# Two attention blocks on one core: another order of the projections, 128 steps of maxima ahead of the loop, sums that stay in one PSUM bank

## The chip, the core and the metric

The kernel runs on one core of a Trainium2 chip. A core has five engines that work side by side, each through its own instructions in order: PE (matrix products; its weight loads stand in the profile as PEld), DVE (vector), ACT (scalar functions and copies), POOL (a slower vector engine) and SP, which here issues the transfers. Results of PE land in PSUM, eight banks of 128 rows by 512 numbers. The metric is device time in microseconds (us): 1739.64 us, the median of three runs (1739.52 to 1739.67).

## The reference

Two independent attention blocks, A and B, on inputs of 2048 rows by 640 columns, 32 heads of 20 columns each. A looks at eight earlier rows (dilation 2) for each row; B looks at all rows:

```python
# A: idx = pos - 2 * arange(8), masked where idx < 0
qkv = (x @ wqkv) ...                                  # both blocks: [2048, 3 * 640]
logits = einsum("bhsd,bhswd->bhsw", q, kg) * scale    # A: 8 gathered keys per row
o = einsum("bhsw,bhswd->bhsd", softmax(logits), vg)   # A
scores = einsum("bhqd,bhkd->bhqk", q, k) * scale      # B: 2048 x 2048 per head
o = einsum("bhqk,bhkd->bhqd", softmax(scores), v)     # B
out = concatenate([oA @ wo_A, oB @ wo_B], axis=-1)
```

## The kernel before

**Products.** Numbers in float32 are split into a rounded part and a rest (`parts`, two instructions on two engines), and a product is three passes (`PASSES`) over five blocks of 128 rows: 15 matrix products for one output tile of 128 rows. Two products of at most 64 rows each run in the two row halves of PE at the same time; a "pair" below is such a couple, of 512 columns for B's scores and 320 for A's values and outputs.

**Before the loop.** PE first makes A's q and k (16 row tiles by 512, 256 and 512 columns), then B's k and q (40 tiles of 15 products of 512 columns), then the v of A and of B (64 tiles of 320 columns, all but the first eight and the last four in row halves). Beside the v's stand 52 steps (`LEAD`) of B's maxima. POOL begins A's attention as soon as A's first q and k rows are back from memory, paced by `a_pace`.

**B's loop.** B is worked in 32 units of 4 heads by 512 queries, each of 16 key blocks: 512 steps. A step has (1) scores, two pairs of 62 rows by 512 columns, and for each of the four tiles an exponential on ACT (tile `e`); (2) maxima for a later unit, two pairs of 60 rows by 512 columns, reduced by DVE (tile `mx`), either a pair at once or each half alone; (3) the values ("PV"), four plain-float32 products of 32 columns each side by side, which the trace shows as eight records `ps_st<-e,vb`. The maxima of a whole unit go through POOL (`mtr`) and memory and come back as two more rows of q, so that the scores are already reduced by their maximum. PV sums two steps in a bank; ACT copies the bank out (`more`, the first one of a unit `braw`), and POOL adds it to the unit's sum (`braw<-braw,more`). At a unit's end its row sums go to memory, DVE takes the reciprocal (`sm`), it comes back spread over the rows (`rb`), POOL multiplies, and the result goes to `ot_b`.

**What sets the order.** PE, ACT and DVE follow a string, `ORDER`, token by token: `S` two score halves, `M` and `N` a pair of maxima, `Y` one score half beside one half of maxima, `H` three pairs of A's output product, `V` the end of a step with its PV; the digits are PSUM banks. The last 24 steps (`TAIL`) follow a plain loop. A's attention on POOL is given out by `begin` at each `V`: POOL's instructions are added until their own estimate, `gp.us`, passes the step's number times `STEP` plus `AHEAD`. An A row tile takes four score units (multiply `akv<-akv,aq`, then adds), a softmax with two small DVE operations, four value units (multiply `akv<-akv,al`, then adds into `ao`), five transpositions on DVE (`turn<-ao`), a way through memory, and a split on POOL (`aot`); then PE can multiply it by the output weights. `after(n, ...)` puts an operation n steps later into its engine's order.

All engine instructions are issued in one helper, L71 of the kernel before and L64 of the changed one, so rows are told apart by tile names.

## Time and profile before

| | us |
|---|---|
| median of the runs | 1739.64 |
| span of the profiled execution | 1736.3 |
| up to the first PV | 458.5 |
| from the first PV to the last (512 steps) | 1229.6 |
| from the last PV to the end | 48.2 |

The profiled execution's own time is its span, 1736.3 us; the median of the runs lies 3.3 us above it. In the page, busy time is the time in which an engine has an instruction running; neighbouring instructions overlap in their ends, so the mean of one is longer than the distance from one start to the next. The records of PE end where the profiler models their end.

### The profile page before, as it was taken

The page shows a single profiled execution, that of the slowest core. Times are in us where ns is not written, and L with a number is a line of the kernel's source. Part 1 is how long each engine was busy: PE and PEld are TensorE (multiplying, and loading weights), DVE is VectorE, ACT ScalarE, POOL GpSimd, SP SyncE. Part 2 cuts the span into 40 slices and gives each one's busy share as a digit, 9 for nine tenths or more (in the row PEclk, how much of TensorE's full clock was granted, in tenths as well). Part 3 has the DMA queues.
Part 4 walks back from the last instruction along what each step waited for, and adds up shares of the span by engine and source line. Part 5 has one row for each costly group of instructions (what it writes and reads, how often), then busy time and mean ns, then how long its engine had stood idle before and what let it go on. Part 6 is the DMA issues. An engine that isn't in the chain of part 4 may idle for free.

```text
span 1736.3 us, 34687 instructions
## 1 busy us (share of the span) xinstructions
PE 1724.5 (99%) x12711; PEld 1006.0 (58%) x12711; DVE 1348.7 (78%) x1825; ACT 1338.9 (77%) x2658; POOL 1266.2 (73%) x1122
## 2 busy tenths in 40 slices
PE   9999999999999999999999999999999999999999
PEld 8988889999545544444344444444444455434569
DVE  3113223988799999999999999999999999999300
ACT  4323224232699999999999999999999999999981
POOL 0000950999899999999999999999999963544242
PEclk9999999999999999999999999999999999999999
DMA  6347878866754365345436434542643532111123
GB/s 227 119 139 239 304 261 273 259 204 187 199 151 125 96 161 153 93 136 158 135 95 173 126 119 127 170 135 88 158 143 106 147 95 61 46 36 53 33 76 113
DMA packets 194436, 248.29 MB, mean 143 GB/s; under 512 B 89309, under 2 KB 114397, under 8 KB 193273
## 3 DMA queue, kind: packets, MB, share of 16 engines
q1 hardware_dynamic: 193688, 245.41, 47.1%
q8 instruction: 100, 1.64, 0.4%
q14 instruction: 72, 0.58, 0.1%
q10 hardware_dynamic: 576, 0.66, 0.1%
HBM read 181.08 MB, written 64.91 MB: 142 GB/s over the span
## 4 chain that ended last, share of the span: by engine, by line
PE 90%; POOL 4%; DVE 2%; ACT 1%; DMA 1%; issue 1%; SPq 0%; POOLq 0%; ACTq 0%; DVEq 0%
PE ps_st L71 90%; POOL akv L71 2%; DVE mx L71 1%; ACT e L71 1%; POOL xn L71 1%; DMA stg<-wv_b 0%; SPq L71 0%; POOL ww L71 0%; POOL xl L71 0%; POOL ao L71 0%; ACT more L71 0%; DMA vb_d<-ve 0%; POOL al L71 0%; DMA s_d<-sm 0%; DMA rb<-s_d 0%
## 5 line engine op out<-in xcount | busy, mean ns | idle before, releaser
L71 DVE TENSOR_REDUCE mx<-ps_st 128x1 f32<-128x512 f32 (+1 forms) x1504 | 1227.6, 875 | 57.3 <-PE ps_st L71 47.8
L71 ACT ACTIVATE e<-ps_st 128x512 f32<-128x512 f32 x2048 | 1066.7, 627 | 30.7 <-PE ps_st L71 16.8
L71 PE MATMUL ps_st<-bk,bq 60*128 60x512 f32 x2048 | 553.4, 436 | 1.0 <-ACT ve L71 0.5
L71 PE MATMUL ps_st<-bq,bk 62*128 62x512 f32 x2048 | 548.7, 433 | 5.6 <-ACT ve L71 3.0
L71 PE MATMUL ps_st<-e,vb 128*32 128x512 f32 x4096 | 543.0, 604 | 0.4
L71 PEld LDWEIGHTS ps_st<-bq,bk 62*128 62x128 f32 x2048 | 274.8, 184 | 403.3 <-ACT e L71 246.5
L71 POOL TENSOR_TENSOR braw<-braw,more 128x512 f32<-128x512 f32 x224 | 288.2, 1287 | 85.5 <-ACT more L71 85.1
L71 PEld LDWEIGHTS ps_st<-bk,bq 60*128 60x128 f32 x2048 | 257.1, 184 | 108.7 <-DVE mx L71 61.2
L71 POOL TENSOR_TENSOR akv<-akv,aq 128x1280 f32<-128x1280 f32 x64 | 188.9, 2951 | 166.4 <-DVE w L71 166.3
L71 POOL TENSOR_TENSOR akv<-akv 128x640 f32<-128x640 f32 (+3 forms) x304 | 282.2, 928 | 14.4
L71 ACT COPY ro<-ps_st 128x320 f32<-128x320 f32 (+2 forms) x172 | 73.7, 463 | 171.1 <-PE ps_st L71 122.7
L71 PE MATMUL ps_st<-ww,xn 64*128 64x320 f32 (+1 forms) x1776 | 187.1, 309 | 0.0
L71 PEld LDWEIGHTS ps_st<-ww,xn 64*128 64x128 f32 (+1 forms) x1776 | 175.7, 186 | 14.6 <-ACT e L71 8.3
L71 PEld LDWEIGHTS ps_st<-e,vb 128*32 128x32 f32 x4096 | 82.1, 108 | 149.0 <-issue 75.4
L71 POOL TENSOR_TENSOR akv<-akv,al 128x1280 f32<-128x1280 f32 x64 | 151.6, 2368 | 0.2
L71 ACT COPY more<-ps_st 128x512 f32<-128x512 f32 x224 | 136.3, 609 | 3.5 <-PE ps_st L71 1.5
L71 PE MATMUL ps_st<-xn,w 128*128 128x512 f32 x480 | 115.8, 390 | 0.0
L71 PEld LDWEIGHTS ps_st<-xn,w 128*128 128x128 f32 x480 | 90.1, 188 | 19.3
L71 ACT CAST pr<-ps_st 128x512 fp32r<-128x512 f32 x40 | 23.5, 587 | 98.8 <-PE ps_st L71 96.0
L71 PE MATMUL ps_st<-ww,aot 64*128 64x320 f32 x960 | 99.7, 308 | 0.0
L71 DVE TENSOR_TENSOR pr<-ps_st,pr 128x512 fp32r<-128x512 f32 x40 | 27.6, 691 | 86.7 <-ACT pr L71 86.7
L71 PEld LDWEIGHTS ps_st<-ww,aot 64*128 64x128 f32 x960 | 90.3, 186 | 5.8 <-POOL ao L71 0.6
(65 smaller groups left out, 1062.5 us busy)
## 6 DMA issues: line engine op xcount, KB each, us to landing
akv<-ka_d SPq DMA_DIRECT2D x128, 320.0 KB
akv<-va_d SPq DMA_DIRECT2D x128, 320.0 KB
kb_d<-pr SPq DMA_DIRECT2D x20, 512.0 KB
qb_d<-pr SPq DMA_DIRECT2D x20, 512.0 KB
bk<-kb_d SPq DMA_DIRECT2D x16, 640.0 KB
bq<-qb_d SPq DMA_DIRECT2D x64, 160.0 KB
stg<-xb SPq DMA_DIRECT2D x16, 512.0 KB
rb<-s_d SPq DMA_DIRECT2D x128, 64.0 KB
```

Source lines behind the costliest of these rows:

```text
L71: return self.tc.keep_in_program_order(op(*a, **k))
```

## The change

- **Order ahead of the loop.** B's k and q come first (full rows). Then one sequence of 48 groups in row halves (`f_tokens`, 30 pairs each): B's v (16 groups of 320 columns), and A's q, k and v together as 1920 columns in pieces of 512, 512, 512 and 384 (32 groups; the weights are brought in twice, for two column blocks of x each). Beside them stand 128 steps (`LEAD`) of maxima as whole pairs, two of them to every 15 narrow pairs, three to every 15 of A's. The splits of A's weights and x use POOL for the rest.
- **A's attention** starts with the loop; nothing of it is issued before. `STEP` is 2.32 instead of 2.36. The five transpositions of a row tile are issued 1 to 5 steps after the tile is handed over (which is one A unit after its last sum), instead of 20 to 24.
- **PV** adds up the 16 steps of a unit in one bank; ACT copies the bank once, into a fixed place (`misc`). The additions on POOL go. The reciprocal of the row sums is issued 3 steps after the load it needs, instead of 7 or 8.
- **Loop.** All 512 steps follow a new `ORDER`, with `F` for one pair of an output group (A's 16 groups, then the first 4 of B's 16). Eight places hold exponentials instead of six. The maxima of 384 steps are left for it, 1158 `Y` and 189 `M` in the first 480 steps; before, 460 steps of maxima.
- **Tail.** Eight more groups of B's output and the last eight tiles follow the last PV. The last unit's row sums are spread by one product with a selection matrix and inverted in PSUM's full width on DVE.

The order in which the built programs have their instructions shows it at three places. First POOL, where A's attention begins. Before, right behind the constants (`mask`, `ve`, `neg`, `zero`):

```order
L71 AFFINE_SELECT mask<-mask 128x256
L71 MEMSET ve 128x347 x4
L71 MEMSET neg 64x128
L71 MEMSET zero 7x640
L71 TENSOR_TENSOR akv<-akv,aq 128x1280
L71 TENSOR_TENSOR akv<-akv 128x2x320
L71 TENSOR_TENSOR akv<-akv 128x2x160
```

In the changed kernel, behind the splits of A's last weights and the eighth unit of maxima:

```order
L64 TENSOR_TENSOR w<-stg,w 128x3x128
L64 TENSOR_TENSOR akv<-stg,akv 128x2x128
L64 TENSOR_TENSOR w<-stg,w 128x3x64
L64 TENSOR_TENSOR akv<-stg,akv 128x2x64
L64 CAST mtr<-mtr 128x32
L64 TENSOR_TENSOR mtr<-mtr 128x32
L64 TENSOR_TENSOR akv<-akv,aq 128x1280
L64 TENSOR_TENSOR akv<-akv 128x2x320
```

All 64 score units and 64 value units of A now stand behind the eighth unit's maxima, which end the work ahead of the loop.

Second ACT, in the middle of the loop, over a unit's end. Before (`e` are exponentials, `more` and `braw` the copies out of PV's bank):

```order
L71 COPY more<-ps_st 128x512
L71 ACTIVATE e<-ps_st 128x512 x6
L71 COPY more<-ps_st 128x512
L71 ACTIVATE e<-ps_st 128x512 x8
L71 COPY more<-ps_st 128x512
L71 ACTIVATE e<-ps_st 128x512 x8
L71 COPY braw<-ps_st 128x512
```

In the changed kernel (exponentials into `pbuf` and `big`, eight of each in turn):

```order
L64 ACTIVATE pbuf<-ps_st 128x512 x8
L64 ACTIVATE big<-ps_st 128x512
L64 COPY misc<-ps_st 128x512
L64 ACTIVATE big<-ps_st 128x512 x7
L64 ACTIVATE pbuf<-ps_st 128x512 x8
L64 ACTIVATE big<-ps_st 128x512 x8
```

One copy for 64 exponentials is left of eight.

Third DVE, around an A row tile's transpositions in the changed loop:

```order
L64 TENSOR_REDUCE mx_6419<-ps_st 128x2
L64 STREAM_TRANSPOSE turn<-ao 128x128
L64 TENSOR_REDUCE mx_6419<-ps_st 128x1 x4
L64 STREAM_TRANSPOSE turn<-ao 128x128
L64 TENSOR_REDUCE mx_6419<-ps_st 128x1 x2
L64 STREAM_TRANSPOSE turn<-ao 128x128
L64 TENSOR_REDUCE mx_6419<-ps_st 128x1 x3
L64 STREAM_TRANSPOSE turn<-ao 128x128
L64 TENSOR_REDUCE mx_6419<-ps_st 128x1
L64 TENSOR_REDUCE mx_6419<-ps_st 128x2
L64 RECIPROCAL sm<-sm 128x16
```

They stand between the reductions of the maxima, as before, about one to a step; but the first is now issued one step after the tile is handed over.

The diff, cut to what the prediction speaks of (of the two `ORDER` strings a line or two):

```diff
-LEAD = 52
-TAIL = 24
+LEAD = 128
+NP = 8
...
-STEP = 2.36
+STEP = 2.32
...
+    def p_tile(t):
+        s = t % NP
+        v = pbuf[:, s].bitcast(F32) if s < 4 else pside[0][:, (s - 4) * 1024:(s - 3) * 1024]
+        return v.rearrange("p (r c) -> p r c", r=2)
...
+    def m_pair(n):
+        m = m_two()
+        for r in range(2):
+            m_matmul(*m[1:], r, psb[:, n + r])
+        m_reduce(*m[1:], None, n)
+        m_done(m)
...
+        after(2, sp.dma_start, sm, s_d[0].rearrange("j (p c) -> j p c", c=16))
+        after(5, dve.reciprocal, sm, sm)
+        after(6, sp.dma_start, s_d[1].rearrange("j (p c) -> j p c", c=16), sm)
+        after(7, bcast)
+        after(9, gp.tensor_tensor, raw, raw, misc[:, 512:], ALU.mult)
+        if then:
+            after(10, then)
+        else:
+            after(11, out)
...
+    def b_pv(i, ns):
+        u, kb = divmod(i, NKB)
+        if kb == 0:
+            accs[u] = psb[:, ns[0]]
+            acc_n[0] = ns[0]
+        acc = accs[u]
+        for j in range(GH):
+            pe.matmul(acc[32 * j:32 * j + 32, :], vs[u // NQC][:, kb, j * VC:j * VC + 32], P[i][j % 2][:, j // 2],
+                      start=(kb == 0), stop=(kb == NKB - 1))
+        del P[i]
+        if kb == NKB - 1:
+            raw = misc[:, :512]
+            act.copy(raw, accs.pop(u))
+            if u < NU - 1:
+                normalize(raw, u, (lambda: out_last(u % NQC, raw)) if u // NQC == NG - 1 else None)
...
-            while any(u[1] >= 4 and v_rows[0] <= u[0] for u in UNITS[n:n + 3]) or c == 4 and len(done_a) > 1:
+            while c == 4 and len(done_a) > 1:
...
-            job(turn_jobs, 20 + k, part, k)
+            job(turn_jobs, 1 + k, part, k)
...
-        if ready_a or not turned or turned[0][0] > now[0]:
+        if not turned or turned[0][0] > now[0] or f_done[0] < turned[0][1] // 2 * 2:
...
+    def f_tokens(lhs, rhs, n, ns):
+        for second in range(2):
+            for k in range(KC):
+                for i, (wi, xi) in enumerate(PASSES):
+                    for r in range(2):
+                        w = r ^ second
+                        rows = slice(r * HALF, r * HALF + HALF)
+                        pe.matmul(psb[:, ns[w], :n], lhs(w, xi, k)[rows], rhs(wi, k)[rows],
+                                  start=(second == 0 and k == 0 and i == 0), stop=(second == 1 and k == KC - 1 and i == 2))
+                    yield
...
+    def oa_group(p, half, ns):
+        assert ready_a[0] >= 2 * p + 2, (p, ready_a)
+        yield from f_tokens(lambda w, xi, k: aot[w][:, xi, k], lambda wi, k: WO[half][wi][:, k], 320, ns)
...
+    for ms in ((5, 6, 7, 8), (9, 0), (1, 2), (3, 4)):
+        for n in range(NQC):
+            for m in ms:
+                if g1 < 4:
+                    p = first[g1]
+                else:
+                    p = bank()
+                    kq_matmuls(p, m, n, range(KC))
+                kq_end(p, m, n)
+                tick()
...
+    groups = [lambda ns, n=n, h=h, a=a: v_group(n, h, a, ns) for n in range(4) for h in range(2) for a in range(2)]
+    groups += [lambda ns, gi=gi, n=n, a=a: a_group(gi, n, a, ns) for gi in range(8) for n in range(gi // 4 * 2, gi // 4 * 2 + 2) for a in range(2)]
...
+    for e in range(0, len(groups), 2):
+        wd = 320 if e < 16 else A_COLS[(e - 16) // 4 % 4 + 1] - A_COLS[(e - 16) // 4 % 4]
+        two = [groups[e + o]((2 * o, 2 * o + 1)) for o in range(2)]
+        for second in range(2):
+            for o in range(2):
+                for k in range(3 * KC):
+                    if k in ((0, 8) if e < 16 else (0, 5, 10)):
+                        m_pair(4 + 2 * (m_next[0] % 2))
+                        spend(0.228)
+                    next(two[o])
+                    spend(0.0135 + wd * 0.000417)
+                if second:
+                    next(two[o], None)
...
+    f_left = [lambda ns, p=p, h=h: oa_group(p, h, ns) for p in range(NT // 2) for h in range(2)]
+    f_left += [lambda ns, qc=qc, a=a, h=h: ob_group(qc, a, h, ns) for qc in range(NQC - 1) for a in range(2) for h in range(2)]
...
-        acc = accs[u]
-        for j in range(GH):
-            pe.matmul(acc[32 * j:32 * j + 32, :], stacks[g][2][:, kb, j * VC:j * VC + 32], P[i][j % 2][:, j // 2],
-                      start=(part == 0), stop=(part == 1))
-        del P[i]
-        if part == 0:
-            return
-        del accs[u]
-        if n == 0:
-            raws[u] = sb.tile([128, 512], F32, tag="raw", bufs=3, name="braw")
-            act.copy(raws[u], acc)
-        else:
-            more = spare[n % 2][:, n // 2 % 2]
-            act.copy(more, acc)
-            after(2, pool, raws[u], raws[u], more, ALU.add)
-        give(acc)
-        if kb == NKB - 1:
-            last = g == NG - 1
...
-        if done_a and done_a[0][0] <= 0 and len(turned) + len(turn_jobs) < 2 and not loads and i > 10:
+        if done_a and done_a[0][0] <= 0 and len(turned) + len(turn_jobs) < 2 and not loads:
             a_turn(*done_a.pop(0)[1:])
         turn_parts()
         gp.us = max(gp.us, (i - 1) * STEP)
-        while i >= A_FROM and gp.us < i * STEP + AHEAD:
...
-        "Y07S61M2Y45V0Y71S26M3Y05V7Y06M3S52Y71V0Y26M3S75VY71M5S24S03N17V2Y06S15Y34VM0S74Y56V3Y70S21N46VY70M4S12S63N07V1"
...
+        "Y10Y23S45M6S10M2S45M6S10M2S45V1S67Y04Y23VS56M3S70VM5S23S47VS02M5Y43VY07S25Y46VY03M5S72VY40Y37S25VY64Y03S72V"
...
+        "F50FFFFY34FFY26FFFY37FFY42FFFY36Y74Y23FFY67FFFY42FFY36FFFY74FFM2FFFM6VS45M2Y60Y74VY25Y63S70VY42Y56S37VY04Y52"
...
+        if kind == "F":
+            if group is None:
+                group = f_left.pop(0)(ns)
+                f_at = 0
+            next(group)
+            f_at += 1
+            if f_at == 6 * KC:
+                next(group, None)
+                group = None
+        elif kind == "V":
+            begin(i)
+            b_pv(i, ns)
...
-    loop[1] = False
-    for i in range(NS - TAIL, NS + LAG):
-        begin(i)
-        if i < NS:
-            b_qk(i)
-        if i % 2:
-            b_pv(i - LAG - 1)
-            b_pv(i - LAG)
-            if fill:
-                fill.pop(0)()
...
+    whole[0] = True
+    while due or f_left:
         tick()
-        if fill:
-            fill.pop(0)()
-    pairs = [wide(), wide()]
-    last = [p for j in range(2) for w in pairs for p in (w[:, j], bank())]
...
+    pe.matmul(end[7], ident, raw, start=True, stop=True)
+    for n in range(1, 7):
+        out_matmuls(n, range(KC - 1))
+    dve.reciprocal(misc[:, 512:], end[7])
+    dve.tensor_tensor(raw, raw, misc[:, 512:], ALU.mult)
+    out_rows(qc, raw, (sp, act))
+    out_matmuls(7, range(KC - 1))
+    parts(chunk(OB[qc], 0, KC - 1), chunk(OB[qc], 1, KC - 1), ob_raw[qc][:, :512])
...
```

More of the change, by code (lines that the diff above doesn't have):

```diff
@@ L292, in attention_pair @@
     tick()
[L293 to L296 removed]
+    for k in range(KC):
+        xb_piece(1, k, 1)
     tick()
[L298 to L304 removed]
+    ident = const.tile([128, 128], F32, name="ident")
     gp.memset(ident, 0.0)
@@ L1165, in attention_pair @@
[L1165 to L1169 removed]
+        if f_left and (len(f_left) > 4 or ob_ready[0] == qc):
+            fb = [n for n in range(8) if n != acc_n[0]]
+            for _ in f_left.pop(0)(fb[len(f_left) % 3 * 2:len(f_left) % 3 * 2 + 2]):
+                pass
```

1238 lines of the change are left out of this document (525 added, 713 removed).

## The prediction

> **What bounds the kernel now.** I read the page's first part, then the windows by stage, then who waits for PE's banks, then PE's own starts.
>
> ```profile
> span 1736.3 us, 34687 instructions
> PE 1724.5 (99%) x12711; PEld 1006.0 (58%) x12711; DVE 1348.7 (78%) x1825; ACT 1338.9 (77%) x2658; POOL 1266.2 (73%) x1122
> ```
>
> PE's 99% is a record of modelled ends. The stages say more (columns: window, length, then busy time and count of PE, PEld, DVE, ACT, POOL, granted clock, share of DMA, GB/s):
>
> ```profile
> 0.00:458.00 458.00, 453.20 (x3309) 398.51 (x3311) 210.89 (x229) 140.44 (x255) 221.87 (x199) 1.00 0.68 219
> 458.00:1688.00 1230.00, 1226.51 (x9102) 563.55 (x9102) 1134.20 (x1590) 1189.90 (x2385) 1034.10 (x914) 1.00 0.41 116
> 640.00:1400.00 760.00, 759.32 (x5654) 342.64 (x5656) 740.65 (x1031) 741.93 (x1491) 735.52 (x638) 1.00 0.47 134
> 1688.00:1736.00 48.00, 44.80 (x308) 43.92 (x300) 3.60 (x7) 8.54 (x19) 10.20 (x10) 1.00 0.36 110
> ```
>
> The loop's edges are the first and last start of PV (count, shortest/median/longest in ns, first to last start):
>
> ```profile
> L71 PE MATMUL ps_st<-e,vb x4096: 592/593/619, 458.5 to 1688.1; 128*32 128x512 f32 x196
> ```
>
> So 458.5 us lie ahead, 1229.6 in it, 48.2 behind. Ahead of the loop and behind it PE alone is full (weight loads 87% and 92% busy). In the middle of the loop DVE, ACT and POOL are all 97% busy: four engines at their limit, and the clock is full. The waits there (640 to 1400; in total, times, longest):
>
> ```profile
> PEld ps_st L71 <- ACT e L71: 211.1, 341, 0.9
> PEld ps_st L71 <- DVE mx L71: 116.7, 241, 0.9
> ...
> PEld ps_st L71 <- POOL ao L71: 0.6, 2, 0.3
> ```
>
> PE takes turns waiting for banks that ACT and DVE must empty, never over 0.9 us; for POOL next to never. What PE needs if it never waits comes from distances between starts. Full rows of 512 and of 256 columns (windows, PE alone), the narrow mix, then a stretch of the loop (start, length, operation):
>
> ```profile
> 160.00:260.00 100.00, 100.00 (x440) 1.00 0.83 286
> 70.00:90.00 20.00, 20.00 (x168) 1.00 0.50 142
> ```
>
> ```profile
> 350.05 0.64 PE L71 MATMUL ps_st<-bk,bq 60*128 60x512 f32 x4
> 350.52 1.93 PE L71 MATMUL ps_st<-ww,xn 64*128 64x320 f32 x24
> 352.29 0.60 PE L71 MATMUL ps_st<-ww,xl 64*128 64x320 f32 x6
> 352.73 0.66 PE L71 MATMUL ps_st<-bk,bq 60*128 60x512 f32 x4
> ...
> 849.41 1.07 PE L71 MATMUL ps_st<-e,vb 128*32 128x512 f32 x8
> 850.40 0.50 PE L71 MATMUL ps_st<-bk,bq 60*128 60x512 f32 x2
> 850.75 0.62 PE L71 MATMUL ps_st<-bq,bk 62*128 62x512 f32 x3
> 850.99 0.45 PE L71 MATMUL ps_st<-bk,bq 60*128 60x512 f32 x1
> 851.37 1.07 PE L71 MATMUL ps_st<-e,vb 128*32 128x512 f32 x8
> ```
>
> 440 products of 512 columns in 100 us are 0.227 each, 168 of 256 in 20 us 0.119. From 350.05 to 352.73, 2.68 us, pass two pairs of 512 and 15 of 320: with 0.228 a wide pair, a narrow one takes (2.68 - 0.46) / 15 = 0.148. PV takes 0.99 (849.41 to 850.40). The pair behind it takes 0.35 and the one ahead of the next PV 0.38, where neighbours stand 0.24 apart: about 0.2 more per PV.
>
> So the loop before needs of PE: scores 512 x 0.456 = 233, maxima 460 x 0.456 = 210, PV 512 x 1.19 = 609, A's outputs 480 x 0.148 = 71, other products 30: 1153 us. It took 1229.6, 1.066 times as much.
>
> **The change part by part.** *Ahead of the loop.* PE's need is B's k and q 600 x 0.227 = 136, B's v 480 pairs x 0.148 = 71, A's 720 pairs of 512 x 0.228 = 164 and 240 of 384 x 0.174 (between the two widths) = 42, maxima 128 x 0.456 = 58: 471. By the same rows the kernel before needs 435 of its 458.5 (A's q and k 240 x (0.227 + 0.119 + 0.227) = 138, B's 136, 62 tiles of v 137, maxima 24), so 24 are start and stalls. I keep these 24: 495, **37 later**. Of this 76 x 0.456 = 35 are maxima brought forward; the loop gets them back. DVE's 256 reductions lie beside PE:
>
> ```profile
> L71 DVE TENSOR_REDUCE mx<-ps_st 128x2 f32<-128x1024 f32 x544 | 657.0, 1216 | 31.5 <-PE ps_st L71 29.8
> L71 DVE TENSOR_REDUCE mx<-ps_st 128x1 f32<-128x512 f32 x960 | 619.8, 681 | 25.8 <-PE ps_st L71 18.0
> L71 ACT COPY more<-ps_st 128x512 f32<-128x512 f32 x224 | 136.3, 609 | 3.5 <-PE ps_st L71 1.5 <-POOL braw L71 1.4 <-issue 0.2
> L71 ACT ACTIVATE e<-ps_st 128x512 f32<-128x512 f32 x2048 | 1066.7, 627 | 30.7 <-PE ps_st L71 16.8 <-ACT e L71 0.3
> ```
>
> 657.0 / 544 = 1.21 each: three in 15 wide pairs are 3.6 us against PE's 4.1, hidden; beside 384 columns PE has 3.3, so DVE sets those 16 stretches, 5 us, inside the 24. A's weights are brought in twice, 4.9 MB more beside some 100 MB in that window (219 GB/s), and asked for a group or more ahead, 8 us: nothing, unless a transfer comes later than that, which then costs its lateness.
>
> *Copies and sums of PV.* ACT loses 224 copies (136.3 us, 0.27 a step), POOL 224 additions (below). If all of ACT's copies were on the path they would be worth 136 us; if PE never waits for what they delay, nothing. ACT's load falls from 2.39 to 2.15 us a step (4 x 1066.7 / 2048, and the rest), DVE's maxima from (960 x 0.646 + 440 x 1.21) / 488 = 2.36 to (1158 x 0.646 + 189 x 1.21) / 480 = 2.03. Both cease to bind at 2.40. I take their worth as less waiting where nothing else binds: half of the 6.6%.
>
> *A's attention on POOL* is the term that decides:
>
> ```profile
> L71 POOL TENSOR_TENSOR braw<-braw,more 128x512 f32<-128x512 f32 x224 | 288.2, 1287 | 85.5 <-ACT more L71 85.1
> L71 POOL TENSOR_TENSOR akv<-akv 128x640 f32<-128x640 f32 (+3 forms) x304 | 282.2, 928 | 14.4
> L71 POOL TENSOR_TENSOR akv<-akv,aq 128x1280 f32<-128x1280 f32 x64 | 188.9, 2951 | 166.4 <-DVE w L71 166.3
> L71 POOL TENSOR_TENSOR akv<-akv,al 128x1280 f32<-128x1280 f32 x64 | 151.6, 2368 | 0.2
> L71 POOL TENSOR_TENSOR ao<-ao,akv 128x640 f32<-128x640 f32 x48 | 75.0, 1563 | 2.0
> L71 POOL TENSOR_TENSOR braw<-braw,rb 128x512 f32<-128x512 f32 x32 | 41.1, 1285 | 29.4 <-DMA rb<-s_d 25.1 <-ACT e L71 4.1 <-issue 0.2
> L71 POOL TENSOR_TENSOR aot<-back,aot 128x640 fp32r<-128x640 f32 x16 | 24.9, 1559 | 1.3
> L71 POOL TENSOR_TENSOR ao<-akv 128x640 f32<-128x640 f32 x16 | 24.9, 1559 | 0.5
> L71 POOL TENSOR_TENSOR al<-al,am 128x256 f32<-128x256 f32 x32 | 23.6, 739 | 0.0
> L71 POOL TENSOR_TENSOR al<-akv 128x64 f32<-128x64 f32 x64 | 20.5, 321 | 4.8
> ```
>
> 288 us go, but the 222 us that POOL had done by 458 now start with the loop. In the changed program A's first multiplication stands at step 4 and its last at step 364. Between them POOL has 282 + 189 + 152 + 75 + 25 + 24 + 21 of A's attention, 22 of 32 normalizations (28), 14 of 16 splits (32 with their casts) and some 25 in small ones: 850 us, **2.36 a step**. From 640 to 1400 it did 735.5 in 760 us, 97%; at that rate the 360 steps take 878, 2.44 each, slower than the 2.40 of before. PE needs only 2.16 there (scores 0.456, 0.8 x 0.456 of maxima, PV 1.19, 12 groups x 30 x 0.148 over 364 steps). POOL can hold PE up in two ways: `F` groups stand 4 to 30 steps behind the split of their second tile, and DVE's transpositions, issued 1 to 5 steps after the handover, wait for POOL's `ao` with the maxima behind them, whose banks PE wants. Before, 20 steps hid that. So I let POOL set these steps: 9 us for the first four, then 878.
>
> *The other 148 steps.* The loop's PE need is 233 + 175 (384 steps of maxima) + 609 + 600 x 0.148 = 1106; 785 of it falls in the first 364 steps, so 321 are left, 70 of them in the last 32 steps, which have no maxima. 251 x 1.033 + 70 = 329.
>
> *Tail.* Eight groups of 30 products (240 x 0.148 = 36) and eight tiles of 15 (18) are 54, the selection product 1 (PV's 0.99 is also plain float32 over 512 columns), and 3 as in the 48.2 of before, 44.8 of it products: 58, 10 more. DVE's reciprocal grows from 16 numbers to 512:
>
> ```profile
> L71 DVE RECIPROCAL sm<-sm 128x16 f32<-128x16 f32 x32 | 7.8, 243 | 1.3 <-DMA sm<-s_d 1.3
> L71 DVE RECIPROCAL am<-am 128x32 f32<-128x32 f32 x16 | 5.5, 343 | 0.0
> ```
>
> 100 ns for 16 more numbers make 3.3 us for 512 (an estimate); with the transfer behind it this lies beside 7 x 12 products, 12 us. Without that cover the tail is up to that 3.3 longer.
>
> *Sum.* 495 + 9 + 878 + 329 + 58 = 1769 us of span against 1736. The median lay 3.3 above the span; with 3 more, **1772 us**, 1.9% slower.
>
> [...]
>
> **The rivals.** *POOL doesn't bind* (18%). For it: before, PE's weight loads waited 0.6 us for POOL in 760 although POOL was just as full, and A's last `F` groups stand 20 steps or more behind their splits. Then the loop takes PE's 1106 at the old loss: 1179, and 495 + 1179 + 58 + 3 = 1735, 0.3% faster. Against it: POOL's 2.36 a step is above the 1179 / 512 = 2.30 that this gives; it decides from where POOL's work a step passes PE's pace.
>
> *PE hardly waits at all* (4%). With ACT at 2.15 and DVE at 2.03 the loop falls to PE's need: 1106, in all 1662. It wants POOL out of the way too, 2.36 a step.
>
> *Waits pile up on DVE* (16%). Two waits of DVE for POOL stand in the whole trace before, 2.85 us each:
>
> ```profile
> DVE am L71 <- POOL al L71: 5.7, 2, 3.8
> ```
>
> If each of 16 row tiles costs one of these, less the 1.2 us that a pair in the next banks covers, 16 x 1.65 = 26 come on top: 1798. [...]
>
> *The change isn't what it says* would be a lead in which DVE, not PE, sets the pace; its price is the 5 us above, and it stays inside the forecast.
>
> **How the numbers follow.** Forecast 62%: 1772, its own range 1754 (POOL at its full 850) to 1790. Rivals 18, 4 and 16%. The range 1733 to 1794 takes in the first rival's 1735 and leaves out the second and half of the third, 12%. Under 0.2% (3.5 us) this kernel's measurement tells nothing. Faster: 11 of the first rival's 18 and the second, 15%; same: 7 and 2 of the forecast, 9%; slower 76%.
>
> **What would show it.** Right: first PV near 495; POOL over 95% busy from there for some 360 steps, ending near 1385; PE's span per step about 2.4 in that time and about 2.2 behind it; DVE waiting for POOL (`turn`, `am`) and PEld for DVE or POOL's `aot` in waits longer than 0.9 us; ACT and DVE below 90%; 58 us behind the last PV. Wrong: POOL with gaps while PE runs at 2.3 or less a step (the first rival), a first PV far from 495 (PE's need mis-sized, or a transfer late in the lead), or PE's long waits on transfers.

## The result: 1842.3 us, 5.9% slower

The changed kernel takes 1842.34 us (median of four runs, 1841.33 to 1843.40), the kernel before beside it 1739.58: a ratio of 1.0593, with a 95% interval of 1.0578 to 1.0608. The prediction said 1772, and 1794 at most. The profile after, first its page:

```profile
span 1839.8 us, 35673 instructions
PE 1741.9 (95%) x13253; PEld 989.4 (54%) x13253; DVE 1370.9 (75%) x1915; ACT 1216.3 (66%) x2410; POOL 974.3 (53%) x898
```

PE is no longer full. The stages of the changed kernel (columns as in the prediction), cut at the first and last PV:

```profile
0.00:508.00 508.00, 491.26 (x4033) 421.31 (x4033) 369.37 (x357) 129.65 (x263) 81.45 (x107) 0.99 0.51 161
508.00:1781.00 1273.00, 1195.97 (x8858) 514.87 (x8858) 994.85 (x1552) 1076.92 (x2126) 885.36 (x783) 0.96 0.48 134
1781.00:1839.00 58.00, 54.69 (x370) 53.18 (x362) 6.71 (x7) 9.72 (x22) 7.51 (x8) 0.99 0.28 90
518.50:1455.00 936.50, 864.06 (x6302) 368.31 (x6304) 765.25 (x1202) 770.10 (x1514) 835.21 (x726) 0.95 0.57 159
```

```profile
L64 PE MATMUL ps_st<-pbuf,vb x2048: 592/593/1062, 508.5 to 1779.5; 128*32 128x512 f32 x187
...
L64 PE MATMUL ps_st<-big,vb x2048: 592/616/1063, 513.0 to 1781.3; 128*32 128x512 f32 x187
```

508.5 us lie ahead of the loop (before 458.5), 1272.8 in it (1229.6), 58.5 behind it (48.2). In the loop every engine has gaps, POOL too: 835 us busy in the 936.5 from A's first to its last multiplication, 89%. And the granted clock is 0.96 where it was 1.00. What DVE waited for in the loop (total, times, longest), and behind it the row for `sm` in the loop of the kernel before:

```profile
DVE mx L64 <- PE ps_st L64: 119.1, 217, 2.3
DVE sm L64 <- DMA sm<-s_d: 106.8, 7, 33.1
DVE w L64 <- DMA stg<-wo_a: 8.8, 2, 7.0
DVE turn L64 <- POOL ao L64: 6.4, 2, 4.2
```

```profile
DVE sm L71 <- DMA sm<-s_d: 0.5, 1, 0.5
```

The long wait is one that the prediction doesn't name: the reciprocal of the row sums waits for their load, with the maxima queued behind it. Two of the seven waits (15.1 and 33.1 us) lie in the last 32 steps, where no maxima are left, and cost nothing. The other five are 58.7 us, at the ends of units 3, 7, 11, 15 and 19, which are the ends of head groups (four units each).

Here is one, in SP's queue at the end of unit 3, whose last PV starts at 663.7 and whose copy starts at 664.9:

```profile
660.61 1.50 SPq L64 DMA_DIRECT2D big<-kb_d  x4
662.21 2.39 SPq L64 DMA_DIRECT2D last<-qb_d  x4
669.46 1.63 SPq L64 DMA_DIRECT2D last<-mdr  x2
675.00 2.83 SPq L64 DMA_DIRECT2D last<-qb_d  x4
...
680.83 0.56 SPq L64 DMA_DIRECT2D s_d<-misc  x1
...
684.49 2.84 SPq L64 DMA_DIRECT2D sm<-s_d  x1
```

At the end of each head group four loads of keys (`big<-kb_d`) for a later group are asked for. The issue records name eight semaphores in turn, 192 issues for each of seven of them and 191 for the eighth, and here a transfer waits for the one issued eight before it: the first key load's last update is at 669.44 and the issue eight behind it at 669.46, the third's at 674.94 and that issue at 675.00. The four key loads hold their semaphores for 9 to 15 us (660.6 to 669.5 for the first, 661.8 to 676.6 for the fourth), and the query loads (`last<-qb_d`) behind them theirs for up to 15. The store of the row sums (`s_d<-misc`), one step behind the unit's end, is asked for 16 us after the copy's start, the load behind it at 684.49, and the reciprocal starts at 690.97.

The five ends are not all alike. At units 7, 15 and 19 the store leaves 15.0, 7.9 and 11.6 us after the copy's start, at all others, unit 11 too, 0.6 to 6. At units 11, 15 and 19 the store itself is slow: the load, which waits for it, is asked for 10 to 11 us behind it, at other units 1.7 to 6.5. Unit 15, where SP waits 9.2 us for the store:

```profile
1169.41 0.55 SPq L64 DMA_DIRECT2D s_d<-misc  x1
...
1180.10 0.32 SPq L64 DMA_DIRECT2D sm<-s_d  x1
```

So the key loads make the sums late in two ways: they hold the semaphores that SP needs, and a store issued close behind two of them takes long (10 to 11 us at these three units). In the first run below, where they stand elsewhere, the load follows the store in 1.7 to 2.8 us at these three units.

PE at the same place (start, length, operation, idle time ahead and its releaser), and the stages around it:

```profile
674.87 1.07 PE L64 MATMUL ps_st<-pbuf,vb 128*32 128x512 f32 x8
...
678.10 0.40 PE L64 MATMUL ps_st<-last,big 62*128 62x512 f32 x1
691.83 0.79 PE L64 MATMUL ps_st<-big,last 60*128 60x512 f32 x1 [13.32 <-DVE mx L64]
...
693.68 1.94 PE L64 MATMUL ps_st<-big,vb 128*32 128x512 f32 x8
```

```profile
680.00:684.00 4.00, 0.00 (x0) 0.00 (x0) 0.00 (x0) 0.00 (x0) 0.65 (x1) 0.58 0.81 201
684.00:688.00 4.00, 0.00 (x0) 0.00 (x0) 0.00 (x0) 0.00 (x0) 3.84 (x3) 0.50 0.99 292
...
696.00:698.00 2.00, 2.00 (x14) 0.57 (x12) 1.59 (x2) 1.19 (x2) 0.48 (x1) 0.58 0.87 313
698.00:700.00 2.00, 2.00 (x18) 0.65 (x14) 2.00 (x5) 1.05 (x3) 2.00 (x2) 1.00 0.13 33
```

PE stands for 13.3 us from 678.5 on. The granted clock (the third figure from a row's end) is 0.58 on average from 680 to 684 and 0.50 behind, so it fell to half some 2 us after PE's last product. The next PV takes 1.94 instead of 1.07. Full speed is back some 6 us after PE has resumed.

**All stops together.** I took PE's products between each two PV's at the prediction's prices as the need of a step (steps count from 0 at the first PV). They add up to 1103 us in the loop (the prediction has 1106), so 170 us are waits. Seven stops, with the slow step behind each, make 90 of them: steps 69, 133, 197, 261 and 324 (the five reciprocals) 16.6, 13.0, 7.8, 13.4 and 17.7, in sum 68.5 (the expectations below have 13.5 and 18.6 for the last two, and so 69.5); steps 3 to 5, where DVE waits for A's output weights, 15.8; step 188, where a transposition waits for POOL's `ao`, 5.8. The other 80 are 7.3% of the need, spread as before (84 of 1146, 7.3% too).

### The profile page after: what moved, and what is told of

It is laid out like the page before. It is cut to its first block, busy times and chain, and to the rows that moved or that the text cites. A ratio compares the mean times of both kernels' runs of the same rounds, so it can differ in the third digit from the quotient of the medians.

```text
span 1839.8 us, 35673 instructions
## 1 busy us (share of the span) xinstructions
PE 1741.9 (95%) x13253; PEld 989.4 (54%) x13253; DVE 1370.9 (75%) x1915; ACT 1216.3 (66%) x2410; POOL 974.3 (53%) x898
## 4 chain that ended last, share of the span: by engine, by line
PE 71%; POOL 12%; DMA 7%; DVE 4%; issue 3%; ACT 2%; SPq 1%; POOLq 0%; ACTq 0%; DVEq 0%
PE ps_st L64 71%; POOL akv L64 9%; DVE mx L64 3%; DMA s_d<-misc 2%; DMA last<-qb_d 1%; DMA sm<-s_d 1%; POOL ao L64 1%; SPq L64 1%; DMA vb_d<-ve 1%; ACT big L64 1%; POOL al L64 1%; POOL big L64 1%; DMA akv<-va_d 0%; DVE w L64 0%; ACT pbuf L64 0%
## 5 line engine op out<-in xcount | busy, mean ns | idle before, releaser
L64 PE MATMUL ps_st<-big,last 60*128 60x512 f32 x2048 | 628.5, 433 | 41.0 <-DVE mx L64 40.5
L64 PE MATMUL ps_st<-last,big 62*128 62x512 f32 x2048 | 605.3, 437 | 37.5 <-DVE mx L64 33.5
L64 ACT ACTIVATE pbuf<-ps_st 128x512 f32<-128x512 f32 x1024 | 543.6, 630 | 93.5 <-PE ps_st L64 86.4
L64 ACT ACTIVATE big<-ps_st 128x512 f32<-128x512 f32 x1024 | 538.5, 637 | 92.5 <-PE ps_st L64 87.1
L64 PEld LDWEIGHTS ps_st<-last,big 62*128 62x128 f32 x2048 | 296.6, 188 | 505.7 <-ACT big L64 140.2
L64 PE MATMUL ps_st<-w,big 64*128 64x320 f32 (+3 forms) x3264 | 379.2, 336 | 12.8 <-ACT ve L64 8.8
L64 PEld LDWEIGHTS ps_st<-w,big 64*128 64x128 f32 (+1 forms) x3264 | 317.7, 188 | 46.3 <-ACT ve L64 9.9
L64 PEld LDWEIGHTS ps_st<-big,last 60*128 60x128 f32 x2048 | 285.8, 187 | 86.1 <-DVE mx L64 52.7
L64 PE MATMUL ps_st<-big,vb 128*32 128x512 f32 x2048 | 278.4, 617 | 0.0
L64 PE MATMUL ps_st<-pbuf,vb 128*32 128x512 f32 x2048 | 274.5, 609 | 0.5 <-DVE mx L64 0.4
```

Of the source, the lines that this page charges most:

```text
L64: return self.tc.keep_in_program_order(op(*a, **k))
```

## The experiments

The first four runs were to tell whether the stops are the whole loss and whether POOL binds behind them.

**Key loads 10 steps later.**

```diff
-                after(1 + d // 2, fn)
+                after(11 + d // 2, fn)
```

> The changed kernel with the four loads of the next key group (big<-kb_d, asked for 1 and 2 steps after a group's last score) moved 10 steps later; nothing else. Theory T: SP's queue is held by these four loads, the row sums' store and load come behind them, and DVE's reciprocal, issued 3 steps after the load, stops the maxima and with them PE at units 3, 7, 11, 15 and 19; those five stops cost 16.6 + 13.0 + 7.8 + 13.5 + 18.6 = 69.5 us beyond PE's need (half-speed clock behind each included), so 1842 - 70 = 1772 (1766 to 1782), and the waits DVE sm <- DMA sm<-s_d of the first 480 steps fall from 58.7 us to under 5. Theory P (POOL sets the pace of A's part): POOL was busy 835 of the 936.5 us from A's first to last multiplication; at the 97% of the kernel before that is 863, so at best 1842 - 73 = 1769: not told apart here. Theory Q (the queue is late whatever the key loads do): 1842 +- 5, waits as before.

Measured: 1803.56 us, ratio 1.0374 (1.0357 to 1.0392): 39 us gained where theory T has 70. The waits of the reciprocal are gone as T says, but ACT has a new one. DVE to 1640 us, then ACT from 1000 to 1345:

```profile
DVE sm L64 <- DMA sm<-s_d: 4.6, 2, 3.6
```

```profile
ACT misc L64 <- DMA ot_b<-misc: 13.9, 2, 7.0
...
ACT misc L64 <- DMA last<-qb_d: 2.9, 1, 2.9
```

The key loads now stand ahead of the store of the finished rows (`ot_b<-misc`). There is one place for the copy of PV's sums, so the next unit's copy waits for that store, and PE for the bank. The stops at steps 207, 271 and 335 cost 8.4, 9.5 and 4.2 us beyond the need, and 5.6 are left at 69. So the cause is as T has it, and the gain that T expects was too high, since the wait moves on.

**Reciprocal 3 steps later.**

```diff
-        after(5, dve.reciprocal, sm, sm)
-        after(6, sp.dma_start, s_d[1].rearrange("j (p c) -> j p c", c=16), sm)
-        after(7, bcast)
-        after(9, gp.tensor_tensor, raw, raw, misc[:, 512:], ALU.mult)
+        after(8, dve.reciprocal, sm, sm)
+        after(9, sp.dma_start, s_d[1].rearrange("j (p c) -> j p c", c=16), sm)
+        after(10, bcast)
+        after(12, gp.tensor_tensor, raw, raw, misc[:, 512:], ALU.mult)
```

> The changed kernel with the reciprocal of the row sums 3 steps later (6 steps after its load instead of 3) and what follows it 3 steps later as well; the key loads stay where they are. T: each of the five waits for the row sums (14.6, 11.0, 6.0, 12.4, 14.7 us) loses what 3 steps take, about 7 us: 24.6 of 58.7 us stay; 34 us of waits and some 5 us of slow clock go: 1842 - 39 = 1803 (1793 to 1812). P: the time doesn't fall below 1769, no other difference. If the reciprocal's place in DVE's order has nothing to do with the stops: 1842 +- 5.

Measured: 1828.99 us, 1.0508 (1.0488 to 1.0528): 13 gained, not 39. The reciprocal's waits in the first 480 steps fall to 30.4 us in five (24.6 were expected); but the finished rows now leave 3 steps later and run into the next unit's copy (step 207: ACT stands 8.8 us ahead of its copy).

**Output weights split later.** Key loads as in the first run, and:

```diff
-    loads += wide_pieces(wo_a, WO, 1, 2, dve.tensor_copy)
+    loads += wide_pieces(wo_a, WO, 1, 12, dve.tensor_copy)
```

> k_later, and in it the second half of A's output weights split on DVE 12 steps after their load instead of 2. T: the stop at steps 3 to 5 (15.8 us, two waits DVE w <- DMA stg<-wo_a of 8.8 us, two slowed splits, slow clock) goes too: 1772 - 16 = 1756 (1748 to 1766). P: POOL then holds the loop at about 863 us for A's part: not below 1769.

Measured: 1799.84 us, 1.0354 (1.0339 to 1.0370). 4 us, not 16: DVE no longer waits for the load, but the splits themselves are slow (steps 15 and 16, where they stand now, lose 6.6 us). Where the rest of the 16 went was not found. In the changed kernel's DVE, first the place where they stood:

```profile
515.97 0.49 DVE L64 CAST w<-stg 128x640 fp32r<-128x640 f32 x1 [1.88 <-DMA stg<-wo_a]
...
525.41 3.04 DVE L64 CAST w<-stg 128x640 fp32r<-128x640 f32 x1 [6.95 <-DMA stg<-wo_a]
528.48 2.04 DVE L64 TENSOR_TENSOR w<-stg,w 128x640 fp32r<-128x640 f32 x1
...
532.17 0.31 DVE L64 CAST w<-stg 128x320 fp32r<-128x320 f32 x1
```

and in this run, DVE and then POOL:

```profile
539.58 2.12 DVE L64 CAST w<-stg 128x320 fp32r<-128x320 f32 x1
541.73 1.74 DVE L64 TENSOR_TENSOR w<-stg,w 128x320 fp32r<-128x320 f32 x1
```

```profile
538.60 2.92 POOL L64 TENSOR_TENSOR akv<-akv,aq 128x1280 f32<-128x1280 f32 x1
```

The same cast of 320 columns takes 0.31 us at one time and 2.12 at another; the slow one starts under a POOL multiplication and ends 0.2 us after it (541.52). The slow cast of 640 columns in the changed kernel, 525.41 to 528.45, likewise starts under a multiplication (525.22 to 528.10) and ends 0.35 us after it. What holds the casts up there, no run shows.

**POOL lightened**, on top of this run:

```diff
-        pool(v, v, L[:, 2 * c:2 * c + 2].unsqueeze(3).to_broadcast([128, 2, H, DH]), ALU.mult)
+        gp.us += 2.37
```

> k_wo without A's 64 multiplications of values by weights on POOL (akv<-akv,al, 151 us; A's half of the output is then a sum of plain values), every other instruction in the same order and the pacing estimate unchanged. T (POOL doesn't bind): the same as k_wo within 5 us. P: POOL's 835 us fall to 684, so A's part is no longer held at 863 us: 25 to 70 us faster than k_wo.

Measured: 1789.15 us, 1.0288 (1.0272 to 1.0303): 10.7 us faster than with all of POOL's work. Neither theory's number. POOL costs something, but isn't the pace.

**Key loads by ACT.** If SP's queue is the trouble, another engine should ask for them.

```diff
-            sp.dma_start(k[r * HALF + r0:r * HALF + r0 + n].bitcast(F32), kb_d[s0:s0 + n, ...])
+            (act if g > 2 else sp).dma_start(k[r * HALF + r0:r * HALF + r0 + n].bitcast(F32), kb_d[s0:s0 + n, ...])
```

> The changed kernel with the four loads of each later key group (from the fourth on) asked for by ACT instead of SP, at the same place in the program. Theory T2: SP lets at most some eight transfers be under way, so slow key loads keep everything behind them in SP's queue; moved later (k_later) they delayed the store of the finished rows, for which the next unit's copy of PV's sums waits because there is one place for it. Off SP's queue they delay neither: waits DVE sm <- DMA sm<-s_d of the first 480 steps under 6 us, no stop at steps 69, 133, 197, 261, 324 nor at 207, 271, 335: 1842 - 69 = 1773 (1766 to 1785). If the queue is slow by itself (or the transfers only share bandwidth): the stops stay, 1800 or more.

Measured: 1840.71 us, 1.0582 (1.0567 to 1.0598): no gain, theory T2 missed by 68 us. What ACT and its queue did at the end of unit 3, and what DVE waited for to 1700 us:

```profile
667.90 0.29 ACTq L64 DMA_DIRECT2D big<-kb_d  x1
668.24 1.58 ACT L64 ACTIVATE pbuf<-ps_st 128x512 f32<-128x512 f32 x3 [6.47 <-DMA ot_b<-misc]
671.59 11.44 ACTq L64 DMA_DIRECT2D big<-kb_d  x2
683.13 2.06 ACT L64 ACTIVATE pbuf<-ps_st 128x512 f32<-128x512 f32 x4 [13.31 <-DMA big<-kb_d]
```

```profile
DVE sm L64 <- DMA sm<-s_d: 10.5, 4, 7.5
```

Of the reciprocal's waits, 58.7 us in the first 480 steps, 10.5 are left: taking the key loads out of SP's queue removes most of them. But now ACT stands still in asking, with its exponentials behind. The eight semaphores are shared by the queues of this program (in the changed kernel's tail, from 1833.17 to 1836.19, eight issues of SP and ACT by turns take the eight once round), so that the wait belongs to whoever asks next. The 6.5 us are for a store that SP had asked for (`ot_b<-misc`); some 11 of the 13.3 us lie in ACT's queue between two key loads (the 11.44 from 671.59), for a key load that ACT itself had asked for. What is left of the reciprocal's waits is mostly unit 15 (7.5 us), where the store leaves 2 us after the copy's start and the load comes 11.6 us behind it: the slow store again.

**Key loads spread out**, at 2, 6, 10 and 14 steps:

```diff
-                after(1 + d // 2, fn)
+                after(2 + 4 * d, fn)
```

> The changed kernel with the four loads of the next key group 2, 6, 10 and 14 steps after the group's last score instead of 1, 1, 2 and 2, still by SP. T2: one slow load at a time holds SP up for a few us only: 1780 (1768 to 1797). If it is the amount that the loads move and not their standing together: as k_later, about 1803, or worse.

Measured: 1804.94 us, 1.0369 (1.0354 to 1.0385). As the second theory has it (about 1803): that they stand apart is worth no more than moving them together. Stops stay at steps 69 (11.1), 207 (6.0) and 324 (6.2).

**ACT for the key loads, and two repairs elsewhere.**

```diff
-    loads += wide_pieces(wo_a, WO, 1, 2, dve.tensor_copy)
+    loads += wide_pieces(wo_a, WO, 1, 6, None, gp)
-        after(1, sp.dma_start, vb_d[s * 128:(s + 1) * 128, half * 16 * VC:half * 16 * VC + c], ve[:, :c])
+        after(1, act.dma_start, vb_d[s * 128:(s + 1) * 128, half * 16 * VC:half * 16 * VC + c], ve[:, :c])
```

> k_act, and with it the second half of A's output weights split by ACT and POOL, 6 steps after the load, instead of DVE, 2 steps after (no split of DVE stands beside a multiplication of POOL any more), and the stores of B's v ahead of the loop asked for by ACT instead of SP. T2: the stop at steps 3 to 5 goes (16 us) and the stop at 201 to 212 us of the lead, where ACT waits for a store of v (10 us with its slow clock): 1773 - 26 = 1747 (1737 to 1762). The first PV comes at about 498 us instead of 508. If POOL sets the pace: not below 1769.

Measured: 1848.45 us, 1.0625 (1.0607 to 1.0643), 101 above T2, with ACT's stops as in the run with the key loads on ACT. The two repairs do what they were meant to: the stop at steps 3 to 5 is gone (22 us of waits in the first 32 steps fall to 13), and the first PV comes at 504.2 instead of 508.5.

**One part of the change alone, in the kernel before**: the reciprocal 3 to 4 steps after its load.

```diff
-            normalize(..., *((2, 3) if last else (5, 8)), ...)
+            normalize(..., *((2, 3) if last else (5, 4)), ...)
```

> The kernel before with one part of the change: the reciprocal of the row sums 3 to 4 steps after its load instead of 7 to 8. T2: here the sums are stored 5 steps after a unit's end, not 1, so behind the key loads anyway; by the trace of before the reciprocal would come about 2 us after the load is asked for at units 11, 15, 19, 23 and 24 and 5 us or more elsewhere: at most five waits of up to 4 us, 1740 + 5 = 1745 (1739 to 1760). If the short distance alone made the changed kernel's stops: 1739 + 60 or more.

Measured: 1752.47 us against 1739.39, 1.0075 (1.0058 to 1.0093). The trace has the wait that the kernel before had not (two of its three waits, 6.8 and 4.1 us, lie ahead of maxima):

```profile
DVE sm L71 <- DMA sm<-s_d: 11.5, 3, 6.8
```

So the short distance alone costs 13 us there, for 10.9 us of waits that count; this is inside T2's range (1739 to 1760) and far from the 60 us more of the other theory. That it costs more in the changed kernel may be because the sums are also stored 1 step after the unit's end and no longer 5, with the key loads just ahead; no run moved the store alone.

**Key loads behind the finished rows** (SP again; with the two repairs of x1):

```diff
-                after(1 + d // 2, fn)
+                after(15 + d // 2, fn)
```

> x1 with the key loads back on SP, but 14 steps later than in the changed kernel: behind the store of the finished rows of their unit and ahead of the next unit's copy. Theory T3 (the transfers share eight places in turn whichever engine asks; a key load holds its place for 9 to 16 us, and the engine that asks for the eighth transfer after it waits): here only A's loads stand behind the key loads. No stop at steps 69, 133, 197, 261, 324 nor at 207, 271, 335: 1842 - 69 - 13 (what x1 shows for steps 0 to 31 and the lead) = 1760 (1750 to 1775). If the loads only push the wait on to whatever stands next in the queue: 1785 or more. P (POOL sets the pace): not below 1769.

> y1 without A's 64 multiplications of values by weights on POOL (151 us; A's half of the output is then a sum of plain values), the order unchanged. T3: what k_wo_light showed, about 11 us (5 to 16) below y1, from waits of POOL's late results, none of them long. P: POOL was the pace: 25 us or more below y1.

> y1 with the reciprocal of the row sums 5 steps after its load instead of 3 (what follows it 2 steps later as well) and the key loads 2 steps later still. T3: as y1 or up to 6 us faster, if single waits for row sums are left in y1: 1757 (1745 to 1775). If the later store of the rows runs into the next unit's copy: up to 20 us slower than y1.

Measured: y1 1808.91 us (1.0401, 1.0378 to 1.0424), y1_light 1787.49 (1.0277, 1.0262 to 1.0292), y5 1800.02 (1.0353, 1.0336 to 1.0370). T3 misses by 49 us: the loads push the wait on again, to the reciprocal of the next unit (steps 149, 213, 277, 341). y1's DVE to 1640 us:

```profile
DVE sm L64 <- DMA sm<-s_d: 34.9, 7, 10.3
```

y5 misses its 1757 by 43. And with POOL lightened y1 is 21 us faster, twice the 11 of T3 and short of the 25 of P, though y1 has no fewer waits than k_wo (144 us beyond the need of its steps, k_wo 133). What POOL's load costs depends on what else stops the loop.

**Time for both places.** Reciprocal 7 steps after the load, key loads as in the first run, x1's repairs, and a second place for the copy. In z1 its room came from the eighth exponential buffer, in u1 from the third buffer of v and outputs:

```diff
-NP = 8
+NP = 7
-            raw = misc[:, :512]
+            raw = misc[:, :512] if u == NU - 1 else pside[0][:, 3072 + u % 2 * 512:3584 + u % 2 * 512]
```

> x1's splits of the output weights and stores of v; the key loads on SP 10 steps later, as in k_later; the reciprocal of the row sums 7 steps after its load instead of 3, and what follows it 4 steps later as well; and two places in turn for the copy of PV's sums instead of one (seven exponential buffers instead of eight make the room). Theory T4: SP's queue is late by up to 16 us once in every group, wherever the key loads stand (k_later, k_spread and y1 only moved the stop to the next one in the queue that has little time), and the changed kernel stops because two things in it have little time: the reciprocal 3 steps behind its load, and the one place of the copy. With both given time the stops go: 1842 - 91 + 6 (a stop for POOL's ao stays) - 4 = 1753 (1744 to 1766), DVE's waits for sm of the first 480 steps under 4 us. If the queue's lateness itself is what costs (the loads of q or k come too late for PE): 1780 or more.

> z1 without A's 64 multiplications of values by weights on POOL (A's half of the output is then a sum of plain values). T4: POOL's load made y1 21 us slower only through SP's queue, which waits for buffers that POOL holds, and so through late row sums; with time for these it is worth 8 us or less: z1 - 4 (z1 - 8 to z1 + 2). P: POOL sets the pace: z1 - 20 or more.

> z1 with the transpositions of A's rows 3 to 7 steps after the handover instead of 1 to 5. The third rival (DVE waits for POOL's ao): 6 us of such waits are in the changed kernel's trace, so z1 - 6 (z1 - 10 to z1 - 2). If they are hidden: z1 +- 2; if the later rows reach the output groups late: up to 10 us more.

Measured: z1 1931.35 us (1.1091, 1.1074 to 1.1107), z1_light 1928.08, z1_t 1942.98. No step in z1's first 480 is over 5 us beyond its need, but its seventh buffer as the last one slowed every step. PE's weight loads waited for exponentials 422 us in these two rows (the changed kernel, in its loop: 301):

```profile
PEld ps_st L64 <- ACT pbuf L64: 237.2, 306, 3.5
PEld ps_st L64 <- ACT big L64: 185.3, 235, 2.3
```

The time of this run can't tell T4 from the rest; its room was taken at the wrong place. At that slower pace POOL's load costs next to nothing (3 us, inside the spread of z1's runs, 1927 to 1931), and later transpositions cost 12.

```diff
-    ones = [sb.tile([128, 16 * VC + 16], F32, tag="r", bufs=3, name="ve") for _ in range(3)]
+    ones = [sb.tile([128, 16 * VC + 16], F32, tag="r", bufs=2, name="ve") for _ in range(2)]
-            raw = misc[:, :512]
+            raw = misc[:, :512] if u % 2 else sb.tile([128, 512], F32, tag="raw", bufs=1, name="raw")
```

> z1 with eight exponential buffers again, as in the changed kernel; the room for a second place of the copy comes from the buffers of v and of the outputs (two instead of three), which can cost some us ahead of the loop. T4 (the stops come from the two places with little time, the reciprocal 3 steps behind its load and the one place of the copy): loop 1272 - 85 = 1187 (1180 to 1198) from first to last PV, in all 1753 (1744 to 1768), DVE's waits for sm of the first 480 steps under 4 us. If the queue's lateness itself costs: 1780 or more.

> u1 without A's 64 multiplications of values by weights on POOL (A's half of the output is then a sum of plain values). T4: POOL's load cost y1 21 us only by way of SP's queue and late row sums; here they have time: u1 - 5 (u1 - 10 to u1 + 2). P (POOL sets the pace): u1 - 20 or more.

Measured: u1 1814.18 us (1.0429, 1.0411 to 1.0446), u1_light 1772.95 (1.0198, 1.0183 to 1.0214). The two differ by 41 us, and all that differs in them is POOL's work. Of u1, DVE to 1700 us and the window of A's part; of u1_light, the same two views:

```profile
DVE turn L64 <- POOL ao L64: 31.4, 9, 8.1
```

```profile
521.70:1431.50 909.80, 872.72 (x6346) 371.80 (x6344) 765.75 (x1205) 777.73 (x1530) 840.91 (x731) 0.97 0.56 163
```

```profile
DVE turn L64 <- POOL ao L64: 3.6, 1, 3.6
```

```profile
521.70:1382.30 860.60, 846.81 (x6276) 360.40 (x6274) 757.31 (x1196) 768.95 (x1516) 691.95 (x667) 0.99 0.59 172
```

The smaller buffers cost 8 us ahead of the loop in both (first PV at 512.3; x1 504.2). In u1 the reciprocals hardly wait any more, 2.2 us in the first 480 steps. In their place DVE's transpositions wait for POOL, nine times, 31.4 us. A's part takes 910 us with POOL 92% busy, and 861 when POOL has 149 us less to do. So T4 falls in its second half: with time at the two places *these* stops are gone, and behind them POOL's work holds the loop after all.

**Is it the transpositions' place, or POOL's pace?**

```diff
-            job(turn_jobs, 1 + k, part, k)
+            job(turn_jobs, 4 + k, part, k)
```

> u1 with the transpositions of A's rows 4 to 8 steps after the handover instead of 1 to 5. T5 (what is left in u1 is the forecast's third rival: DVE's transpositions wait for POOL's ao, 31.4 us in nine waits of up to 8.1 us, with the maxima behind them): 3 steps are some 7 us, so nearly all of these waits go, and with the half-speed clock behind each about 1.3 times as much: 1814 - 40 = 1774 (1765 to 1785), near u1_light's 1773. P (POOL's pace itself): the rows then come late to the output groups instead, PE waits for POOL's splits: 1800 or more.

Measured: 1824.90 us, 1.0493 (1.0453 to 1.0533), 11 slower than u1. T5 falls. DVE's waits for `ao` shrink to 8.4 us, and PE's own grow from 1.2 to 33.6. PE and then DVE, to 1440 us (`big` is where the split rows of A lie):

```profile
PE ps_st L64 <- POOL big L64: 33.6, 8, 13.2
```

```profile
DVE turn L64 <- POOL ao L64: 8.4, 2, 7.4
```

POOL's rows come late to the output groups wherever the wait is put. No version here beats the kernel before; the nearest with the full computation is the one with later key loads and splits, 1799.84.

## Why the prediction was wrong

The direction was right, the size was not: 1842 against 1772, 70 us. The direction is no proof of the reasoning, since POOL, which was to make the kernel slower, did not set its pace. By the prediction's steps:

- **Ahead of the loop: 495, measured 508.5.** PE's need was taken right as far as can be seen, the 24 us of stalls were not; they are 37. Two stretches and a wait show it:

```profile
200.00:220.00 20.00, 12.42 (x134) 12.06 (x132) 9.47 (x8) 2.55 (x6) 0.00 (x0) 0.83 0.52 144
...
360.00:380.00 20.00, 17.46 (x144) 14.24 (x142) 14.35 (x15) 3.15 (x8) 9.53 (x12) 0.83 0.47 150
```

```profile
ACT ve L64 <- DMA vb_d<-ve: 29.1, 7, 9.7
```

```profile
369.80 1.08 PE L64 MATMUL ps_st<-w,big 64*128 64x512 f32 x4 [1.62 <-ACT w L64]
```

  In the first, ACT waits for a store of v before it can fill that buffer again, and PE for ACT; the stores by ACT in x1 brought 4 us. In the second, PE waits for the split of A's weights that are brought in a second time. For these the prediction had "nothing, unless a transfer comes later"; the store of v, the larger loss, is not in it.
- **The reciprocal: the step that failed.** The prediction costs it only in the tail. In the loop its distance to the load went from 7 or 8 steps to 3, in DVE's order ahead of the maxima, and that was put at nothing with no cover named. What the runs showed in its place: five waits, 58.7 us, 68.5 beyond PE's need with what follows each. That this is so near the miss of 70 is partly chance: 13.5 of the 70 lie ahead of the loop, and 59.5 in A's part (946.5 us from the first PV to A's last multiplication, 887 predicted), where the forecast had POOL's pace and no stops. The waits shrink when the key loads leave SP's queue (10.5 us left with ACT) and go when the reciprocal has time (2.2 us left in u1). before_r shows that the same part alone costs 13 us even in the kernel before. The trace of before had the numbers: the rows' store and load queue on SP behind key loads that took, in its loop, 4.6 to 15.5 us from issue to the last update of their semaphore, and SP waited for them there as it does now (44.5 us in the changed kernel):

```profile
SPq L71 <- DMA bk<-kb_d: 51.1, 20, 4.9
```

- **The third rival had the engine and the queue right and the releaser wrong.** It let DVE wait for POOL at 16 row tiles, 26 us (from 2.85 us, the mean of two waits of 3.8 and 1.9). In the changed kernel DVE waits for POOL at `ao` 6.4 us in all, and for the load of the row sums 58.7 that count. Its own mechanism appears in u1, at 31.4 us, once the loads are out of the way.
- **POOL as the pace: not seen in the result, and right behind it.** The 850 us are 835 in the trace. But A's part took 936.5 us and not 878, since the stops left POOL with nothing to do: 89%, not 97%. The test is the lightened POOL: 11 us in k_wo and 21 in y1, which both have other stops, 41 in u1, where the reciprocals hardly wait. In u1 A's part takes 910 us at 92%, and with POOL lightened 861, where something else holds it. So "POOL sets these steps" is wrong as the account of this kernel's time; it describes what u1 runs into, some 30 us above the 878 that it gave.
- **The first rival (POOL doesn't bind, 1735)** had the loss nearly right, 7.3% beside the stops where it has 6.6%, and missed the stops. It is what the kernel would take with neither: 508.5 + 1103 x 1.073 + 58.5 + 2.5 = 1753 by these rows (an estimate), above before in any case.
- **The other steps and the tail** hold: 1455 to 1781.3 is 326 us (329 predicted for the steps beside A's part), and 58.5 lie behind the last PV (58). The reciprocal over 512 numbers takes 3.4 us and is hidden there, as said.
- **The output weights** are not in the prediction: six operations on DVE at the loop's start, 15.8 us by their load and by POOL's multiplications beside them.
- **The copies of PV** were to be worth half of PE's waits. The share of waits beside the stops is 7.3% as before: 224 copies fewer on ACT and lighter maxima on DVE bought nothing that can be seen.

What stays open: why a key load takes 7 to 15 us in the changed loop. Its rows move beside A's loads (the 16 transfer engines are 0.60 to 0.75 busy in each 5 us between 660 and 680), and no run changed its shape. In both traces every key load of 40 rows has 11 updates of its semaphore and every one of 22 rows 12, the first of them 0.4 to 1.3 us after the issue; what each of them stands for, no run shows. Nor was a kernel found in which the stops and POOL's load are gone together with the full computation.

## What to carry to other kernels

When an instruction that needs a load is put closer behind it, price the whole queue that the load and the store ahead of it stand in at its worst moment, not at its mean: here it was late by up to 16 us, once in 64 steps. DVE works through its instructions in order here, and that lateness was paid by everything behind: at the end of unit 3 the maxima stood behind the reciprocal and PE for 13.3 us behind them. And a wait that was moved along the shared queue here only found the next place with little time (k_later, y1); it went when both such places had time (2.2 us left in u1), and then the next limit showed itself, here POOL.

## What the runs showed of the hardware

- A stop of PE cost more than its length. After 13.3 us the granted clock stood at 0.50, and the next PV took 1.94 us instead of 1.07; its step took 3.44 us (693.68 to 697.12), one with as many products ahead of the stop 1.90 (674.87 to 676.77). Waits of up to 0.9 us, of which the loop before is full, left it at 1.00; a wait of 1.62 us from 368.2, with one of 0.92 behind it, went with half the clock for a while (1.00 from 368 to 370, 0.50 from 370 to 376). In both places the clock fell some 2 us after the end of PE's last product (678.5 and 368.2).
- A cast of 320 columns on DVE between two places in SBUF took 0.31 us with no POOL multiplication beside it and 2.12 under one; one of 640 columns 0.49 and 3.04. Two reductions out of PSUM beside that multiplication of k_wo (538.60 to 541.52) took 1.28 us together from 538.38, and the two ahead of it 1.28 from 535.92.
- The transfers that ACT asked for in k_act stopped ACT, with its exponentials, until earlier ones had landed, whoever had asked for those: 6.5 us for a store that SP had asked for, 13.3 us of which some 11 were for a key load of its own.
- One of eight exponential buffers less is worth 117 us here (z1 against u1, which differ otherwise only in where the second copy lies and in one buffer of v and outputs).
